# Clustered attention with a fused feed-forward block on one core: first weight sums made ahead of the clips, part of the second ones behind the first products

## The chip, the cores and the metric

The kernel runs on one core of a Trainium2 chip. The metric is the device time of one execution in microseconds (us), lower is better. The core has five engines with queues of their own: TensorE (PE in the profile, its weight loads PEld), VectorE (DVE), ScalarE (ACT), GpSimd (POOL), and SyncE (SP), which issues most transfers. Each takes its instructions in program order; they meet through semaphores.

## The reference

Attention in which a query sees only the keys of its own cluster, followed by a feed-forward block:

```python
q_assign = np.argmax(np.einsum('bhsd,hcd->bhsc', q_n, c_n), axis=-1)   # 16 clusters per head
k_assign = np.argmax(np.einsum('bhsd,hcd->bhsc', k_n, c_n), axis=-1)
mask = q_assign[:, :, :, None] == k_assign[:, :, None, :]
scores = np.where(mask, scale * np.matmul(q, k.transpose(0, 1, 3, 2)), -1e9)
attn = softmax(scores)                       # over the keys, 1e-9 in the denominator
x = np.matmul(attn, v) as (3072, 512)        # 4 batches x 768 tokens, 8 heads x 64
h = x @ w_in                                 # (512, 2048)
g = h * np.clip(h + 3.0, 0.0, 6.0) / 6.0
return g @ w_out                             # (2048, 512)
```

Everything arrives as 64-bit numbers; the kernel rebuilds 32-bit weights from the two halves of each.

## The kernel before

**Stages.** The sixteen pairs of heads are split in two. Pairs 0 to 7 (batches 0 and 1) run as full attention with a cluster mask in steps `n` = 0 to 95, two steps per turn of the loop from line 1284 on. Pairs 8 to 15 run later, with rows sorted by cluster, woven between feed-forward work by a hand-written plan (`late_plan`). The feed-forward block works on 12 blocks of 256 tokens (`B * NHC`); for each there are eight `up` items (first product, item `i` handles the hidden columns `i` and `i + 8` of 128 each) and seven `down` parts (second product, parts 0 to 6).

**Fewer products from sums.** From the second block on, both products use a scheme of seven half-size products in place of eight, which needs sums of weight blocks. The *first weight sums* (`make_first_sums(i)`, one call for each of the eight items) are four VectorE subtractions of 128x256 on `w_in_sb`: three go to a tile `tx` that is stored in DRAM as `td[:, i]` and read again for each later block, the fourth overwrites a block of `w_in_sb`. The first token block still multiplies with the plain `w_in_sb`, so the overwriting subtraction of an item has to come after the first block's use of it. The *second weight sums* (`weight_sums(0..7)`, two halves each of T1, T2, T4 and T3, in this order) are subtractions of 128x1024 on `w_out_sb`; T3 overwrites its source. All 12 blocks' `down` parts use them: part 0 and 1 use T2, part 2 T1, part 3 T3, part 6 T4.

**The first block's items.** Its `up` items run inside the attention loop, the last six of its parts behind it. An item does eight TensorE products into a PSUM tile `ph` (line 597), a lift on ScalarE (line 499), a clip on VectorE (line 502), and with every second item four GpSimd sums of the result (line 635). A counter, `want`, lets them start at n = 60, 64, 70, 74, 80, 84, 90 and 94 (items 0 to 7), and part 0 of `down` at n = 100. Within a turn the item goes ahead of the `prep` steps of the next pair: `turn` (transposes `pqk`, line 320, copied out on ScalarE, line 326) at r = 0 and 2 of the pair's twelve steps, then `cluster_scores`, `route`, and `route_turn` (transposes `po`, line 379). In this stage the tiles `ph`, `pqk`, `pcs`, `pr`, `po` and `pd` share two PSUM slots.

**VectorE in the loop.** Behind the items of a turn come `decode` steps, a list that `share(n, r)` works off: for each of 32 weight chunks `split` (line 232), `join` (238), `power` (248), `rest` (254) and `total` (259), and behind these the eight `weight_sums`. Every sixth step a reciprocal and a multiplication divide one half of a pair's result (lines 473 and 474, `pd` read out of PSUM). GpSimd adds up exponentials (lines 430 and 433, 128x768). Raw weight chunks are loaded by SP with three buffers (line 215).

**The first block's `down` parts.** Each part is eight TensorE products of 128x256 (line 684) into bank `X` or `Y`. `end()` of a part has the eviction: part 1 adds `X` to `y0` (line 691), which frees `X` for part 4; part 3 evicts `Y`, parts 4 and 6 the rest. For the first block the calls of `make_first_sums` stand in front of these evictions: items 7 and 6 at part 0, 5 at part 1, 4 at part 2, 3 and 2 at part 4, 0 at part 5, 1 at part 6.

Of the kernel before, what the change touches and what calls it, by code (L numbers as in the profile page):

```python
# [12 lines left out]
ALU = mybir.AluOpType  # L13
# [15 lines left out]
NFT = DFF // P  # L29
# [90 lines left out]
def fast_path(ctx, tc, ok, q, k, v, centroids, moe_w_in, moe_w_out, out):  # L120
# [3 lines left out]
    nc = tc.nc  # L124
# [53 lines left out]
    st = {}  # L178
# [329 lines left out]
    HF, HC = NFT // 2, DM // 2  # L508
# [30 lines left out]
    def wi(s, t, i):  # L539
        f = t * HF + i  # L540
        return w_in_sb[:, s * HK : (s + 1) * HK, f * P : (f + 1) * P]
# [8 lines left out]
    def make_first_sums(i):  # L550

        tx = txp.tile([P, 3, HK, P], F32, name="tx")
        t1, t2, t4 = (tx[:, k] for k in range(3))
        b11, b12, b21, b22 = wi(0, 0, i), wi(0, 1, i), wi(1, 0, i), wi(1, 1, i)
        for out_, in0, in1 in ((t1, b12, b11), (t2, b22, t1), (t4, b21, t2), (b12, b22, b12)):
            nc.vector.tensor_tensor(out=out_, in0=in0, in1=in1, op=ALU.subtract)  # L556
        nc.sync.dma_start(td[:, i], tx)
        if i < 2:
            st["tx", HF + i] = tx

    def token_sums(b, m):

# [15 lines left out]
    def ffn_items(b):  # L578
        def up(m, i):
            u = (b * NHC + m) * HF + i  # L580
            g = g_sb[:, 0:4, i]
            got = {}

            def begin():
                raise_gates()
                load_block()
                if u >= HF:
                    first_sums(u + 2)
                    halved(b, m, u, i, got)

            def end():
                if u < HF:
                    ph = psum_m.tile([P, 512], F32, name="ph", tag="m")
                    for t in range(2):
                        f = t * HF + i
                        for kt in range(NKT):
                            nc.tensor.matmul(
                                ph[:, t * HC : (t + 1) * HC], lhsT=w_in_sb[:, kt, f * P : (f + 1) * P],
                                rhs=st["xb", b, m][:, kt], start=(kt == 0), stop=(kt == NKT - 1),
                            )  # L600
# [92 lines left out]
        def down(m, part):  # L693
            def keep(chunk, half, y, queue=nc.sync):
                queue.dma_start(out_v[b, 2 * m + chunk][:, half * HC : (half + 1) * HC], y)

            def multiply(second):
                if part < 2:
                    h = range(part * HF // 2, (part + 1) * HF // 2)
                    if second:  # L700
                        product(st["X"], 1, 5, st["T2"], False, True, False, h)
                    else:
                        product(st["X"], 0, 0, wb[0][0], True, False, False, h)
                    return
                kind, bank, half, w = (
                    (4, "Y", 0, st["T1"]), (1, "Y", 1, st["T3"]),
                    (2, "X", 0, wb[1][0]), (6, "Y", 0, wb[1][1]), (3, "Y", 1, st["T4"]),
                )[part - 2]
                h = range(second * HF // 2, (second + 1) * HF // 2)
                product(st[bank], half, kind, w, part == 2, part in (3, 4, 6), part > 3, h)  # L710

            def begin():
                raise_gates()
                if part == 0:
                    st["X"] = psum_m.tile([P, DM], F32, name="X", tag="m")
                    st["y0"] = yp.tile([P, DM], F32, name="y0", tag="y0")
                elif part == 2:
                    st["Y"] = st.get("psum_y", psum_m).tile([P, DM], F32, name="Y", tag="m")
                    st["y1"] = yp.tile([P, DM], F32, name="y1", tag="y1")
                multiply(0)  # L720

            def end():
                multiply(1)
                if part == 0:
                    finish()
                if (b, m, part) == (B - 1, NHC - 1, 6):
                    st["good"] = nc.values_load(ok[0:1, 0:1], min_val=0, max_val=1)
                if part == 4:
                    token_sums(*divmod(b * NHC + m + 1, NHC))
                if (b, m) == (0, 0):  # L730
                    for i in ([HF - 1, HF - 2], [5], [4], [], [3, 2], [0], [1])[part]:
                        make_first_sums(i)
                y0, y1 = st["y0"], st.get("y1")
                if part == 1:
                    nc.scalar.copy(out=y0[:, HC:], in_=st["X"][:, HC:])
                    add(y0[:, HC:], y0[:, HC:], st["X"][:, 0:HC])
                elif part == 3:
                    add(y1[:, 0:HC], y0[:, HC:], st["Y"][:, HC:])
                    add(y1[:, HC:], y1[:, 0:HC], st["Y"][:, 0:HC])
                    keep(1, 1, y1[:, HC:])  # L740
                elif part == 4:
                    nc.scalar.copy(out=y0[:, 0:HC], in_=st["X"][:, 0:HC])
                    keep(0, 0, y0[:, 0:HC])
                elif part == 6:
                    add(y1[:, 0:HC], y0[:, HC:], st["Y"][:, HC:])
                    keep(1, 0, y1[:, 0:HC])
                    add(y0[:, HC:], y0[:, HC:], st["Y"][:, 0:HC])

                    keep(0, 1, y0[:, HC:], nc.scalar if st["last"] else nc.sync)

            return [begin, end]

# [475 lines left out]
    per_batch = NKT * per_pair  # L1228
    total = FIRST * per_pair
    lag_v, lag_d = 2, 4  # L1230
    up_first = NFT // 2

    decode = [step for i in range(NW) for step in decoding_steps(i)]
    decode += [lambda i=i: weight_sums(i) for i in range(8)]
    READY, DECODED = per_batch + 2 * lag_d, 2 * per_batch

    def share(n, r):  # L1240
# [9 lines left out]
    st["early"] = st["free"] = True  # L1250
    st["last"] = st["moving"] = False
    fill, checks = [], []
    st["done"] = 0

    def check_all():
        now, checks[:] = checks[:], []
# [7 lines left out]
    with tc.manual_schedule():  # L1264
# [19 lines left out]
        for n in range(0, total + lag_d + 2, 2):  # L1284
# [10 lines left out]
            m = n - lag_d + 1  # L1295
# [5 lines left out]
            if r == 6:  # L1301
                load(g + 2, "q", "k")
                load(g + 1, "v")
            want = min(max(n + 2 - READY, 0) * up_first // (DECODED - READY) - st["done"], len(fill) // 2)
            st["done"] += want
            for i in range(max(len(prep), want)):
                if i < want:
                    fill.pop(0)()
                    fill.pop(0)()
                if i < len(prep):  # L1310
                    prep[i]()
            if n < total:
                for step in decode[: share(n, r)]:
                    step()
# [388 lines left out]
```

## Time and profile before

| what | value |
|---|---|
| median of 3 runs | 959.21 us (956.59 to 961.89) |
| the profiled execution | 959.56 us, its span 957.8 us |
| TensorE clock granted | 0.998 of full speed |
| PE busy in 0 to 130 us, 130 to 280, 280 to 957.8 | 126.56, 140.31, 662.78 us |
| VectorE busy in the same stretches | 108.50, 131.89, 353.97 us |
| first block's items on PE | 136.4 to 238.8 us |
| first block's `down` parts on PE | 242.7 to 270.3 us |

The program's span is 1.8 us shorter than the time measured for the same execution. The first row of the table is what later runs are compared with. A row of the views that follow has a start in us, a duration in us, the engine, the line, the operation, and output<-input; in square brackets stands how long the engine sat idle before it and what released it.

### The profile page before, as it was taken

The page shows a single profiled execution, that of the slowest core. Times are in us where ns is not written, and L with a number is a line of the kernel's source. Part 1 is how long each engine was busy: PE and PEld are TensorE (multiplying, and loading weights), DVE is VectorE, ACT ScalarE, POOL GpSimd, SP SyncE. Part 2 cuts the span into 40 slices and gives each one's busy share as a digit, 9 for nine tenths or more (in the row PEclk, how much of TensorE's full clock was granted, in tenths as well). Part 3 has the DMA queues.
Part 4 walks back from the last instruction along what each step waited for, and adds up shares of the span by engine and source line. Part 5 has one row for each costly group of instructions (what it writes and reads, how often), then busy time and mean ns, then how long its engine had stood idle before and what let it go on. Part 6 is the DMA issues. An engine that isn't in the chain of part 4 may idle for free.

```text
span 957.8 us, 17621 instructions
## 1 busy us (share of the span) xinstructions
PE 929.6 (97%) x6358; PEld 725.5 (76%) x6358; DVE 594.4 (62%) x1306; ACT 349.8 (37%) x731; POOL 576.3 (60%) x1302
## 2 busy tenths in 40 slices
PE   8999999999899999999999999999999999999997
PEld 5444445555698798787897988888888799999996
DVE  6789888989977276274483474374471564636261
ACT  6888877765112232222232231241331311202020
POOL 3877767657367577776777878767777160303030
PEclk9999999999999999999999999999999999999999
DMA  7255464350474557456584484654744333323210
GB/s 206 90 133 155 132 176 124 106 145 10 145 223 137 151 159 164 129 130 153 153 198 119 120 204 118 160 155 114 198 142 95 102 96 116 102 72 105 66 57 26
DMA packets 174351, 124.23 MB, mean 130 GB/s; under 512 B 134064, under 2 KB 152496, under 8 KB 174256
## 3 DMA queue, kind: packets, MB, share of 16 engines
q1 hardware_dynamic: 164320, 109.86, 42.7%
q0 software_dynamic: 9216, 12.60, 4.4%
q8 instruction: 52, 0.85, 0.4%
q10 hardware_dynamic: 720, 0.56, 0.2%
q14 instruction: 43, 0.35, 0.1%
HBM read 94.67 MB, written 28.31 MB: 128 GB/s over the span
## 4 chain that ended last, share of the span: by engine, by line
PE 67%; DVE 3%; DMA 2%; issue 1%; ACT 0%; SPq 0%; another core or an unknown queue 0%; ACTq 0%; DVEq 0%
PE Y L684 17%; PE uY L645 15%; PE X L684 12%; PE uX L645 11%; PE pv L1096 3%; PE ps L899 3%; PE ps L1057 3%; DMA piece<-qd 2%; PE pv L1057 1%; PE pd L1120 1%; PE pcs L337 1%; PE rk L981 1%; PE ps L1137 1%; DVE tx L556 0%; DVE w_out_sb L523 0%
## 5 line engine op out<-in xcount | busy, mean ns | idle before, releaser
L433 POOL TENSOR_TENSOR acc<-acc,ex 128x768 f32<-128x768 f32 x64 | 123.3, 1927 | 37.4 <-ACT ex L423 33.9
L1014 POOL DMA_INDIRECT qd<-qn,pos x96 | 96.2, 1002 | 54.8 <-issue 17.5
L1030 POOL DMA_INDIRECT xn<-xsd,pos x96 | 94.3, 982 | 46.0 <-ACT sx L499 24.3
L499 ACT ACTIVATE sx<-g_sb,half_c 128x512 f32<-128x512 f32 x88 | 63.8, 725 | 146.5 <-DVE g_sb L656 126.3
L635 POOL TENSOR_TENSOR g_sb<-g_sb 128x256 f32<-128x256 f32 x52 | 41.8, 825 | 122.1 <-DVE g_sb L502 121.1
L1014 POOL DMA_INDIRECT kvd<-kvn,pos x96 | 96.1, 1001 | 27.3 <-issue 25.4
L1006 POOL MEMSET w_low<- 128x1 f32 x864 | 91.3, 106 | 33.3
L691 DVE TENSOR_TENSOR y<-y,Y 128x256 f32<-128x256 f32 x48 | 20.2, 421 | 132.7 <-PE Y L684 131.9
L684 PE MATMUL X<-w_out_sb,g_sb 128*128 128x256 f32 x384 | 90.4, 382 | 4.0 <-DVE y L691 2.2
L645 PE MATMUL uX<-xb,w_in_sb 128*128 128x128 f32 x704 | 93.0, 275 | 0.0
L684 PE MATMUL Y<-T,g_sb 128*128 128x256 f32 x384 | 88.0, 381 | 0.0
L684 PE MATMUL Y<-w_out_sb,g_sb 128*128 128x256 f32 x384 | 87.7, 380 | 0.0
L645 PEld LDWEIGHTS uX<-xb,w_in_sb 128*128 128x128 f32 x704 | 85.7, 192 | 0.0
L684 PEld LDWEIGHTS X<-w_out_sb,g_sb 128*128 128x128 f32 x384 | 70.9, 190 | 18.5 <-issue 4.0
L684 PEld LDWEIGHTS Y<-T,g_sb 128*128 128x128 f32 x384 | 72.1, 190 | 13.2 <-issue 3.9
L684 PEld LDWEIGHTS Y<-w_out_sb,g_sb 128*128 128x128 f32 x384 | 71.9, 190 | 10.6 <-issue 1.3
L656 DVE TENSOR_TENSOR sx<-uX,sx 128x128 f32<-128x128 f32 x176 | 51.1, 290 | 45.9 <-ACT sx L663 30.8
L400 PE MATMUL ps<-xf 64*128 64x384 f32 x384 | 78.5, 487 | 0.6 <-ACT ex L423 0.6
L423 ACT ACTIVATE ex<-ps 128x768 f32<-128x768 f32 x96 | 72.6, 802 | 4.5 <-PE ps L400 4.5
L443 PE MATMUL pv<-ex,vt 128*64 128x384 f32 x384 | 72.5, 499 | 0.0
L502 DVE SCALAR_TENSOR_TENSOR g_sb<-sx,g_sb 128x512 f32<-128x512 f32 x88 | 63.9, 728 | 3.3 <-ACT sx L499 2.3
L656 DVE TENSOR_TENSOR g_sb<-uY,sx 128x128 f32<-128x128 f32 (+1 forms) x176 | 65.6, 414 | 0.0
(194 smaller groups left out, 1796.7 us busy)
## 6 DMA issues: line engine op xcount, KB each, us to landing
tx<-td SPq DMA_DIRECT2D x86, 384.0 KB
raw<-in_moe_w_in_dram SPq DMA_DIRECT2D x16, 512.0 KB
raw<-in_moe_w_out_dram SPq DMA_DIRECT2D x16, 512.0 KB
xb<-xd SPq DMA_DIRECT2D x12, 512.0 KB
out_dram<-y SPq DMA_DIRECT2D x44, 128.0 KB
qk<-in_q_dram SPq DMA_DIRECT2D x18, 192.0 KB
qk<-in_k_dram SPq DMA_DIRECT2D x18, 192.0 KB
vt<-in_v_dram SPq DMA_DIRECT2D x16, 192.0 KB
```

Of the source, the lines that this page charges most:

```text
L400: nc.tensor.matmul(st["ps", n][:, t, 0:HALF], lhsT=x[r, NCH + j], rhs=x[r, hf * NHC : (hf + 1) * NHC], start=first, stop=last, skip_group_ ...
L423: nc.scalar.activation(out=ex, in_=sc, func=ACT.Exp, scale=SM_SCALE)
L433: nc.gpsimd.tensor_tensor(out=acc, in0=acc, in1=ex, op=ALU.add)
L443: nc.tensor.matmul(pv[t * D : (t + 1) * D], lhsT=vt[:, t, j], rhs=ex[:, t], start=(j == 0), stop=(j == NCH - 1),)
L499: nc.scalar.activation(out=r, in_=h, func=ACT.Relu, bias=half_c, scale=1.0 / 6.0)
L502: nc.vector.scalar_tensor_tensor(out=g, in0=r, scalar=1.0, in1=h, op0=ALU.min, op1=ALU.mult)
L645: nc.tensor.matmul(dst, lhsT=w[:, kt], rhs=x(kt), start=(kt == 0), stop=(kt == HK - 1))
L656: nc.vector.tensor_tensor(out=out_, in0=in0, in1=in1, op=ALU.add)
L684: nc.tensor.matmul(bank[:, half * HC : (half + 1) * HC], lhsT=g_sb[:, kind, i], rhs=w[:, i], start=(first and i == 0), stop=(last and i == ...
L1006: nc.gpsimd.memset(w_low, W_LOW)
L1014: i = nc.gpsimd.indirect_dma_start(out=rows[name, g, t], in_=src, in_offset=None, out_offset=bass.IndirectOffsetOnAxis(ap=pos[:, a, j, t : ...
L1030: nc.gpsimd.indirect_dma_start(out=xn[:, j, t], out_offset=None, in_=rows["xsd", g, t], in_offset=bass.IndirectOffsetOnAxis(ap=pos[:, 0, j ...
```

## The change

1. `make_first_sums(i)` is split: `kept_sums(i)` does the three subtractions into `tx` and stores it, the fourth stays in `make_first_sums`, which calls `kept_sums` only for an item that hasn't had it. `kept_sums` of items 7, 6, 5 and of 4 and 3 is issued in `end()` of the first block's `up` items 0, 1, 2 and 5 (`sooner`), ahead of the item's products and so of its clip in VectorE's queue.
2. The last four `weight_sums` (both halves of T4 and of T3) leave the decode list. T3's halves are made at the end of parts 0 and 1 of the first block's `down`, T4's at the end of parts 2 and 3.
3. In `end()` of the first block's parts, the sums now follow the evictions.
4. The counter `want` gives way to a list of steps, `up_at`. Item 3 goes from n = 74 to n = 72. Where a turn of the loop has two `turn` steps (r = 0: n = 60, 72, 84), the first of them is issued ahead of the item, the second behind it; before, the item was ahead of both.

```diff
+    def subtract(out_, in0, in1):
+        nc.vector.tensor_tensor(out=out_, in0=in0, in1=in1, op=ALU.subtract)
+    def kept_sums(i):
         tx = txp.tile([P, 3, HK, P], F32, name="tx")
         t1, t2, t4 = (tx[:, k] for k in range(3))
-        b11, b12, b21, b22 = wi(0, 0, i), wi(0, 1, i), wi(1, 0, i), wi(1, 1, i)
-        for out_, in0, in1 in ((t1, b12, b11), (t2, b22, t1), (t4, b21, t2), (b12, b22, b12)):
-            nc.vector.tensor_tensor(out=out_, in0=in0, in1=in1, op=ALU.subtract)
+        for sums in ((t1, wi(0, 1, i), wi(0, 0, i)), (t2, wi(1, 1, i), t1), (t4, wi(1, 0, i), t2)):
+            subtract(*sums)
         nc.sync.dma_start(td[:, i], tx)
         if i < 2:
             st["tx", HF + i] = tx
+        st["kept"].add(i)
+    def make_first_sums(i):
+        if i not in st["kept"]:
+            kept_sums(i)
+        subtract(wi(0, 1, i), wi(1, 1, i), wi(0, 1, i))
...
             def end():
                 if u < HF:
+                    for other in sooner.get(u, ()):
+                        kept_sums(other)
                     ph = psum_m.tile([P, 512], F32, name="ph", tag="m")
...
-                if (b, m) == (0, 0):
-                    for i in ([HF - 1, HF - 2], [5], [4], [], [3, 2], [0], [1])[part]:
-                        make_first_sums(i)
                 y0, y1 = st["y0"], st.get("y1")
...
+                if (b, m) == (0, 0):
+                    for i in ([HF - 1, HF - 2], [5], [4], [], [3, 2], [0], [1])[part]:
+                        make_first_sums(i)
+                    if part in (0, 1):
+                        weight_sums(6 + part)
+                    elif part in (2, 3):
+                        weight_sums(2 + part)
...
-    decode += [lambda i=i: weight_sums(i) for i in range(8)]
+    decode += [lambda i=i: weight_sums(i) for i in range(4)]
+    st["kept"] = set()
+    sooner = {0: (7,), 1: (6,), 2: (5,), 5: (4, 3)}
+    up_at = (60, 64, 70, 72, 80, 84, 90, 94, 100)
...
-            want = min(max(n + 2 - READY, 0) * up_first // (DECODED - READY) - st["done"], len(fill) // 2)
-            st["done"] += want
-            for i in range(max(len(prep), want)):
-                if i < want:
-                    fill.pop(0)()
-                    fill.pop(0)()
-                if i < len(prep):
-                    prep[i]()
+            if len(prep) > 1:
+                prep.pop(0)()
+            if n in up_at:
+                fill.pop(0)()
+                fill.pop(0)()
+            for step in prep:
+                step()
```

More of the change, by code (lines that the diff above doesn't have):

```diff
@@ L548, in first_sums @@
             nc.sync.dma_start(tx, td[:, i])
-    def make_first_sums(i):
+    def subtract(out_, in0, in1):
+        nc.vector.tensor_tensor(out=out_, in0=in0, in1=in1, op=ALU.subtract)
+    def kept_sums(i):
         tx = txp.tile([P, 3, HK, P], F32, name="tx")
         t1, t2, t4 = (tx[:, k] for k in range(3))
-        b11, b12, b21, b22 = wi(0, 0, i), wi(0, 1, i), wi(1, 0, i), wi(1, 1, i)
-        for out_, in0, in1 in ((t1, b12, b11), (t2, b22, t1), (t4, b21, t2), (b12, b22, b12)):
-            nc.vector.tensor_tensor(out=out_, in0=in0, in1=in1, op=ALU.subtract)
+        for sums in ((t1, wi(0, 1, i), wi(0, 0, i)), (t2, wi(1, 1, i), t1), (t4, wi(1, 0, i), t2)):
+            subtract(*sums)
         nc.sync.dma_start(td[:, i], tx)
@@ L1230, in fast_path @@
     lag_v, lag_d = 2, 4
-    up_first = NFT // 2
     decode = [step for i in range(NW) for step in decoding_steps(i)]
-    decode += [lambda i=i: weight_sums(i) for i in range(8)]
+    decode += [lambda i=i: weight_sums(i) for i in range(4)]
+    st["kept"] = set()
+    sooner = {0: (7,), 1: (6,), 2: (5,), 5: (4, 3)}
+    up_at = (60, 64, 70, 72, 80, 84, 90, 94, 100)
     READY, DECODED = per_batch + 2 * lag_d, 2 * per_batch
@@ L1252, in fast_path @@
     fill, checks = [], []
-    st["done"] = 0
     def check_all():
```

## The prediction

> **What bounds the kernel now.** I read the page's head first, then TensorE's waits, then its order of time around the change, then VectorE's.
>
> ```profile
> span 957.8 us, 17621 instructions
> ...
> PE 929.6 (97%) x6358; PEld 725.5 (76%) x6358; DVE 594.4 (62%) x1306; ACT 349.8 (37%) x731; POOL 576.3 (60%) x1302
> ```
>
> TensorE is busy for 97% of the span, and no edit removes a product. So the change can win only TensorE's idle time, and only where it touches it, between 130 and 280 us. The list of TensorE's waits (total, times, longest, in us) names what is there to win:
>
> ```profile
> PE X L684 <- DVE y L691: 2.2, 1, 2.2
> PE X L684 <- DVE g_sb L502: 1.8, 1, 1.8
> ...
> PE pqk L320 <- ACT xf L326: 1.6, 2, 0.8
> ...
> PE pqk L320 <- DVE rcp L473: 0.7, 1, 0.7
> ...
> PE uX L645 <- DVE sx L656: 0.4, 1, 0.4
> PE po L379 <- DVE rcp L473: 0.4, 1, 0.4
> ```
>
> In TensorE's order of time these are the places:
>
> ```profile
> 141.39 0.66 PE L320 MATMUL pqk<-ident,qk 128*128 128x128 f32 x4 [0.82 <-ACT xf L326]
> ...
> 173.39 1.09 PE L320 MATMUL pqk<-ident,qk 128*128 128x128 f32 x8
> ...
> 178.22 3.72 PE L597 MATMUL ph<-xb,w_in_sb 128*128 128x256 f32 x16
> 182.69 0.66 PE L320 MATMUL pqk<-ident,qk 128*128 128x128 f32 x4 [0.75 <-DVE rcp L473]
> ...
> 198.76 0.49 PE L379 MATMUL po<-ident_q,one_hot 128*128 128x128 bf16 x6 [0.38 <-DVE rcp L473]
> ...
> 242.73 1.99 PE L684 MATMUL X<-w_out_sb,g_sb 128*128 128x256 f32 x8 [1.82 <-DVE g_sb L502]
> ...
> 253.19 3.62 PE L684 MATMUL Y<-w_out_sb,g_sb 128*128 128x256 f32 x16
> 259.02 1.99 PE L684 MATMUL X<-w_out_sb,g_sb 128*128 128x256 f32 x8 [2.21 <-DVE y L691]
> ```
>
> Together 2.21 + 1.82 + 1.64 + 0.75 + 0.41 + 0.38 = 7.2 us: the most this change can take off TensorE's path. Four of these six waits end on VectorE. Its order of time shows why, and where it has room:
>
> ```profile
> 140.90 0.69 DVE L502 SCALAR_TENSOR_TENSOR g_sb<-g_sb,ph 128x512 f32<-128x512 f32 x1 [2.30 <-ACT g_sb L499]
> ...
> 154.80 0.69 DVE L502 SCALAR_TENSOR_TENSOR g_sb<-g_sb,ph 128x512 f32<-128x512 f32 x1 [2.15 <-ACT g_sb L499]
> ...
> 170.15 0.69 DVE L502 SCALAR_TENSOR_TENSOR g_sb<-g_sb,ph 128x512 f32<-128x512 f32 x1 [1.18 <-ACT g_sb L499]
> ...
> 173.65 0.69 DVE L238 SCALAR_TENSOR_TENSOR wtop<-raw,wtop 128x512 uint32<-128x512 uint32 x1
> ...
> 175.11 2.15 DVE L254 SCALAR_TENSOR_TENSOR wunit<-raw,wunit 128x512 f32<-128x512 uint32 x1
> ...
> 180.08 2.55 DVE L473 RECIPROCAL rcp<-pd 128x384 f32<-128x384 f32 x1
> ...
> 196.16 2.55 DVE L473 RECIPROCAL rcp<-pd 128x384 f32<-128x384 f32 x1
> ...
> 207.57 0.69 DVE L259 TENSOR_TENSOR w_out_sb<-wtop,wunit 128x512 f32<-128x512 f32 x1
> 211.57 0.69 DVE L502 SCALAR_TENSOR_TENSOR g_sb<-g_sb,ph 128x512 f32<-128x512 f32 x1 [3.31 <-ACT g_sb L499]
> ...
> 228.63 0.69 DVE L502 SCALAR_TENSOR_TENSOR g_sb<-g_sb,ph 128x512 f32<-128x512 f32 x1 [0.51 <-ACT g_sb L499]
> ...
> 230.29 2.78 DVE L523 TENSOR_TENSOR T<-w_out_sb 128x1024 f32<-128x1024 f32 x1
> ...
> 239.72 2.35 DVE L523 TENSOR_TENSOR T<-w_out_sb,T 128x1024 f32<-128x1024 f32 x2
> 241.99 0.68 DVE L502 SCALAR_TENSOR_TENSOR g_sb<-g_sb,ph 128x512 f32<-128x512 f32 x1
> 242.59 2.88 DVE L523 TENSOR_TENSOR T<-w_out_sb,T 128x1024 f32<-128x1024 f32 x2
> 245.39 3.41 DVE L523 TENSOR_TENSOR w_out_sb<-w_out_sb 128x1024 f32<-128x1024 f32 x2
> 248.72 2.54 DVE L473 RECIPROCAL rcp<-pd 128x384 f32<-128x384 f32 x1
> ...
> 258.55 0.41 DVE L691 TENSOR_TENSOR y<-y,X 128x256 f32<-128x256 f32 x1
> ```
>
> The reader is to see two things. The clips wait for their lifts, and leave VectorE gaps of 2.30, 2.15, 1.18 and 3.31 us, exactly at the items that get early sums. And between the gaps it has none: from 170.15 to 208 us no row has a bracket, and from 211.57 to 242.67 only 0.51 us is free. Where the first product starts is VectorE's end of that chain (241.99 + 0.68), not TensorE's.
>
> A third fact lies in durations. T1's halves take 2.78 us and T2's 2.35 / 2 = 1.2, for the same shape:
>
> ```profile
> 166.46 3.89 POOL L433 TENSOR_TENSOR acc<-acc,ex 128x768 f32<-128x768 f32 x2 [1.86 <-ACT ex L423]
> 174.89 1.81 POOL L430 TENSOR_TENSOR acc<-ex 128x768 f32<-128x768 f32 x1 [4.53 <-ACT ex L423]
> ...
> 230.18 8.54 POOL L433 TENSOR_TENSOR acc<-acc,ex 128x768 f32<-128x768 f32 x4 [3.33 <-ACT ex L423]
> ```
>
> T1's first half began 0.1 us after a GpSimd add and lasted about such an add (1.81) longer than T2's. The 2.15 us row of line 254 ends 0.56 us after the GpSimd add that had begun just ahead of it at 174.89; its neighbours of the same size take 0.69. So a VectorE operation with both inputs in SBUF, which meets a running GpSimd add, waits for that add to end: 0 to 1.8 us each. All moved sums are of this kind.
>
> **Part by part.**
>
> *Order of `turn` and item (n = 60, 72, 84).* The second `turn` waited for the first one's copy, queued behind the lift: 0.82 us, twice. Now the item's 3.7 us lie between the two, and the copy needs 0.6: minus 0.82 at 60 and at 84. At n = 74 the third `turn` waited 0.75 for the reciprocal; with item 3 gone from there it waits for item 3's clip, long done: minus 0.75.
>
> *Fifteen early subtractions* of 128x256:
>
> ```profile
> L556 DVE TENSOR_TENSOR tx<-w_in_sb,tx x16: 424/425/490, 252.3 to 270.7; 128x256 f32<-128x256 f32 x16
> L556 DVE TENSOR_TENSOR tx<-w_in_sb x8: 413/419/420, 251.8 to 269.8; 128x256 f32<-128x256 f32 x8
> ```
>
> 0.42 + 2 x 0.425 = 1.27 us for one item, 6.3 for five. Alone they fit the gaps (1.27 in 2.30 and 2.15, 1.27 in 1.18, 2.55 in 3.31), so nothing to 0.1 us is the lower end. With a GpSimd add in the way each gap costs up to 1.8 more: 4 x 1.8 = 7.2 less the spare 1.03 + 0.88 + 0.76 = 4.5 us, the upper end. At item 2 I take the waiting case, since the row at 166.46 covers that gap until 170.35: clip at about 170.75 (0.6 later than before, though its lift comes 0.8 earlier). At item 0 and 1 the add ends early enough. The five stores of `tx` join SP's queue ahead of raw weight loads, which wait for VectorE's line 254 anyway and run two chunks (7 us of decoding) ahead; I cost them at nothing, and with the cover gone at one subtraction's delay each, 1.3 us.
>
> *Item 3 at n = 72.* VectorE reaches this clip behind the row at 173.65, so at 174.4 + 0.6 = 175.0. TensorE issues the item at 173.39 - 0.82 + 0.55 = 173.1, ends at 176.8; the lift takes 0.7 more: 177.6. VectorE stands for 2.6 us where it had no gap, and behind it wait six decode steps and the reciprocal: 177.6 + 0.6 + 6 x 0.72 + 0.4 of GpSimd's delay = 182.9 instead of 180.08. The clip no longer comes after it (0.6), so the chain is 2.3 us late from here; its ends are 0 (if line 254's 1.5 us of waiting at 175.11 is saved on top of the other gains) and 3.5.
>
> *Reciprocal at 196.16.* It ends 2.3 later, at 201.0. TensorE is there 0.82 + 0.75 = 1.57 us earlier than its 198.38, so its 0.38 grows to 4.2: the gains so far go into this wait, and TensorE is 2.3 late.
>
> *Item 5 (n = 84).* The lift ended where the clip began, at 211.5, and ends at 211.5 + 2.3 + 0.6 (the `turn` ahead of the item) = 214.4; VectorE is free at 208.3 + 2.3 = 210.6 and needs 2.55, with a GpSimd add 4.4: clip between 214.4 and 215.0, 3.0 late. The 0.51 gap takes its share: 2.5 late. T1's two waits (2.78 - 1.21 = 1.57 each) were almost the longest possible; shifted against GpSimd by 1 us I take the mean, half of 1.8, which gives back 1.4. The first product starts 1.1 us late; its ends are minus 4.6 (VectorE in time: 2 x 0.82, 0.75, 0.38 and 1.82 all won) and plus 6.6 (rival C).
>
> *T3 and T4 behind the first products, evictions first.* 2.88 + 3.41 us leave the queue ahead of the reciprocal at 248.72 and of the add at 258.55, and so do sums of items 7, 6 and 5. New queue from the first product's start: reciprocal and multiplication 3.1, two overwriting sums 0.85, T3's first half 1.7, the small set-up operations 1.9, then the add, ending at 8.0 us. Part 4 needs it at 253.19 + 3.45 - 242.73 = 13.9: the 2.21 us vanish. T3's second half is done by 10.2 and needed at 12.2, T4's by about 17, needed at 20.9; these covers are thin for T3 only.
>
> *Part 6.* Item 1's sums (1.7 us) now stand behind the last eviction and ahead of the next block's additions, where they were ahead of both: these start about 2.5 us after the block's first product instead of 2.0, and item 2's reload stands behind item 1's store in SP's queue. The 0.41 us wait stays and grows: I take plus 0.3, ends minus 0.4 and plus 1.
>
> Sum: 1.1 - 2.2 + 0.3 = -0.8 us against 959.56. That execution lies 0.35 above the median, so I name 958.4 for a median. Behind 280 us TensorE hardly waits for this stage, and I carry the shift to the end.
>
> **The rivals.**
>
> *B, all waits go.* VectorE's lateness stays under 1 us because the moved operations meet no adds: minus 5 to 7.2, 952 to 954.2. For it: the sums' length fits the gaps. Against: the gap that item 3 opens, which no earlier work fills.
>
> *C, VectorE becomes the bound of the attention stage.* The early sums lose a whole add at each of four gaps (4.5 us), item 3's gap adds 2.6, and the first product starts 7.1 - 0.5 = 6.6 us late; with 2.2 given back and 0 to 1 for part 6, plus 4.4 to 5.4: 963.6 to 964.6. It decides from 7 us of lateness on. For it: the row at 166.46; against: one add per gap, often over early. The Trainium skill ("SBUF — State Buffer", Who interferes with whom) has the rule behind it: a VectorE instruction with two SBUF inputs and a GpSimd one reading SBUF exclude each other for the whole instruction. The T1 rows agree (2.78 against 1.2).
>
> *D, the wait moves only.* T3's second half misses its 2.0 us of cover, and part 3 waits instead of part 4: plus 1.4, 960.6. GpSimd's sums of item 7 run in that stretch and could hold T3 up.
>
> **How the numbers follow.** Forecast 0.59, B 0.18, C 0.12, D 0.11. I call 0.5% (4.8 us) the least that can be told from no change: under 954.4 faster, over 964.0 slower. B gives 0.17 faster, C 0.09 slower, the rest lies within: 0.74. The range goes from B's middle, 953.8, to short of C, 962.6.
>
> **What would show it.** Right: `pqk` without waits at n = 60, 74 and 84; a gap of 2 to 3 us before item 3's clip; `po` waiting about 4 us for a reciprocal; no wait of `X` for line 691's add. Wrong: the `po` wait under 1 us (B's sign), clips 3 us or more behind their lifts (C), a wait of `Y` for T3 (D), or a moved time in stretches behind 300 us, which nothing here explains.

## The result, and the profile after

| us | kernel before | kernel after |
|---|---|---|
| median (lowest to highest), 7 executions each | 959.23 (956.59 to 961.89) | 954.56 (953.32 to 956.97) |
| the profiled execution | 959.56 | 955.15 |
| its span | 957.8 | 953.4 |

The ratio of after to before is 0.995, with a 95% interval of 0.9933 to 0.9966: 4.7 us less, where 0.8 were forecast. The interval leaves out 1; by the bound that the prediction set for telling a change (0.5%, 4.8 us) it lies just within, and near the lower end of the range.

The list of TensorE's waits in the profile after (total, times, longest, in us) answers to the one shown of before:

```profile
PE ph L607 <- DVE one_hot L357: 2.3, 1, 2.3
...
PE X L694 <- DVE g_sb L502: 1.8, 1, 1.8
...
PE uX L655 <- DVE sx L666: 0.6, 1, 0.6
```

The waits of `pqk` and that of `X` for the late add (line 701 now) are gone, the 1.8 us ahead of the first product are untouched, and 2.3 us are new. In TensorE's order of time (start, duration, waits in brackets):

```profile
140.29 0.60 PE L320 MATMUL pqk<-ident,qk 128*128 128x128 f32 x4
144.62 0.66 PE L320 MATMUL pqk<-ident,qk 128*128 128x128 f32 x4
...
173.17 3.62 PE L607 MATMUL ph<-xb,w_in_sb 128*128 128x256 f32 x16
...
180.97 0.66 PE L320 MATMUL pqk<-ident,qk 128*128 128x128 f32 x4
...
195.35 5.38 PE L607 MATMUL ph<-xb,w_in_sb 128*128 128x256 f32 x16 [2.33 <-DVE one_hot L357]
...
243.69 1.99 PE L694 MATMUL X<-w_out_sb,g_sb 128*128 128x256 f32 x8 [1.82 <-DVE g_sb L502]
...
257.61 1.89 PE L694 MATMUL X<-w_out_sb,g_sb 128*128 128x256 f32 x8
...
275.67 0.68 PE L655 MATMUL uX<-xs,tx 128*128 128x128 f32 x4 [0.65 <-DVE sx L666]
```

The sixteen products at 195.35 took 5.38 us, not 3.72. Windows of 2 us show why: the granted clock (third number from the end) was halved from 196 us to a little over 199.

```profile
194.00:196.00 2.00, 0.65 (x3) 0.63 (x4) 1.93 (x6) 0.00 (x0) 1.47 (x1) 1.00 0.99 320
196.00:198.00 2.00, 2.00 (x7) 1.56 (x6) 1.97 (x3) 0.00 (x0) 0.00 (x0) 0.50 1.34 258
198.00:200.00 2.00, 2.00 (x8) 1.64 (x7) 1.91 (x2) 0.00 (x0) 0.00 (x0) 0.64 1.15 271
```

VectorE's order of time after, at the clips that got early sums, at item 3's clip, and at the one-hots behind it:

```profile
138.44 2.04 DVE L551 TENSOR_TENSOR tx<-w_in_sb 128x256 f32<-128x256 f32 x1
...
141.31 0.68 DVE L502 SCALAR_TENSOR_TENSOR g_sb<-g_sb,ph 128x512 f32<-128x512 f32 x1
...
171.46 0.68 DVE L502 SCALAR_TENSOR_TENSOR g_sb<-g_sb,ph 128x512 f32<-128x512 f32 x1
...
177.55 0.69 DVE L502 SCALAR_TENSOR_TENSOR g_sb<-g_sb,ph 128x512 f32<-128x512 f32 x1 [1.90 <-ACT g_sb L499]
...
182.42 2.55 DVE L473 RECIPROCAL rcp<-pd 128x384 f32<-128x384 f32 x1
...
194.58 0.62 DVE L357 TENSOR_TENSOR one_hot<-pr,mx 128x192 bf16<-128x192 f32 x2
...
197.17 2.55 DVE L473 RECIPROCAL rcp<-pd 128x384 f32<-128x384 f32 x1
...
210.68 2.38 DVE L551 TENSOR_TENSOR tx<-w_in_sb,tx 128x256 f32<-128x256 f32 x2
...
214.23 0.68 DVE L502 SCALAR_TENSOR_TENSOR g_sb<-g_sb,ph 128x512 f32<-128x512 f32 x1
```

The one-hots that in after start at 194.58 stood in before at

```profile
192.31 0.62 DVE L357 TENSOR_TENSOR one_hot<-pr,mx 128x192 bf16<-128x192 f32 x2
```

Where did 4.4 us of span come from? Two steps that both kernels issue in the same order, the turn of `dn` and the first product of the second block's T2, stood in the first profile of before at

```profile
407.05 0.49 PE L1133 MATMUL pdt<-ident,dn 128*128 128x128 f32 x3
...
418.47 0.87 PE L899 MATMUL ps<-ident,piece 128*128 128x128 f32 x6 [1.26 <-ACT xnat L900]
421.73 0.85 PE L337 MATMUL pcs<-xnat,cnT 128*32 128x384 f32 x8 [0.60 <-ACT xnat L900]
434.77 0.84 PE L899 MATMUL ps<-ident,piece 128*128 128x128 f32 x6 [0.56 <-issue]
436.08 1.91 PE L684 MATMUL X<-T,g_sb 128*128 128x256 f32 x8
```

and in that of after at

```profile
405.20 0.49 PE L1147 MATMUL pdt<-ident,dn 128*128 128x128 f32 x3
...
429.60 0.85 PE L913 MATMUL ps<-ident,piece 128*128 128x128 f32 x6 [0.15 <-issue]
430.91 1.91 PE L694 MATMUL X<-T,g_sb 128*128 128x256 f32 x8
```

So after is 407.05 - 405.20 = 1.85 us ahead at the first and 5.17 at the second. Up to 405 us after has gained 1.85, but only 1.3 of it by 296 us; the other 0.6 arose near 300 us, where this profile of before is that much slower than the second one shown below. Another 3.3 came in 30 us of work that no edit touches. At the end the lead is 4.4: in after a second stretch at half clock follows on the wait of 2.09 us at 611 us (a wait, and the windows behind it), which before had too, without such a stretch.

```profile
611.41 0.84 PE L913 MATMUL ps<-ident,piece 128*128 128x128 f32 x6 [2.09 <-DMA piece<-qd]
```

```profile
612.00:614.00 2.00, 2.00 (x18) 1.97 (x17) 0.62 (x2) 0.80 (x1) 1.71 (x5) 0.61 1.09 280
614.00:616.00 2.00, 2.00 (x12) 2.00 (x11) 0.00 (x0) 0.00 (x0) 1.74 (x5) 0.54 1.04 261
```

### The profile page after: what moved, and what is told of

Same layout as the page of the kernel before. It is cut to its first block, busy times and chain, and to the rows that moved or that the text cites. A ratio compares the mean times of both kernels' runs of the same rounds, so it can differ in the third digit from the quotient of the medians.

```text
span 953.4 us, 17615 instructions
## 1 busy us (share of the span) xinstructions
PE 930.6 (98%) x6358; PEld 728.2 (76%) x6358; DVE 595.6 (62%) x1306; ACT 349.7 (37%) x731; POOL 574.6 (60%) x1302
## 4 chain that ended last, share of the span: by engine, by line
PE 69%; DMA 2%; issue 1%; DVE 1%; SPq 0%; POOL 0%; ACT 0%
PE Y L694 17%; PE uY L655 15%; PE X L694 13%; PE uX L655 11%; PE pv L1110 3%; PE ps L913 3%; PE ps L1071 3%; DMA piece<-qd 2%; PE pv L1071 1%; PE pd L1134 1%; PE pcs L337 1%; PE ps L1151 1%; PE rk L995 0%; PE pdt L1147 0%; DVE y L701 0%
## 5 line engine op out<-in xcount | busy, mean ns | idle before, releaser
L645 POOL TENSOR_TENSOR g_sb<-g_sb 128x256 f32<-128x256 f32 x52 | 38.0, 754 | 125.5 <-DVE g_sb L502 124.5
L1028 POOL DMA_INDIRECT kvd<-kvn,pos x96 | 95.6, 996 | 25.7 <-issue 24.7
```

What stands on the lines that cost most here:

```text
L1028: i = nc.gpsimd.indirect_dma_start(out=rows[name, g, t], in_=src, in_offset=None, out_offset=bass.IndirectOffsetOnAxis(ap=pos[:, a, j, t : ...
```

## The experiments

Theory W: the gain is what the removed waits between 130 and 280 us bring, less VectorE's lateness. For the 3.3 us behind 405 us there are two: theory S, that the passage is slow in before whenever it runs and any shift of the stage ahead shortens it, and theory O, that it is a thing of single executions. Each set ran on one chip, with the kernel before beside it; the three sets ran on three chips. All differences are of medians within a set.

| kernel | median, us | before beside it, us | ratio (95%) |
|---|---|---|---|
| order alone | 958.46 | 957.03 | 1.0017 (1.0007 to 1.0028) |
| early sums alone | 952.17 | 957.03 | 0.9959 (0.9945 to 0.9974) |
| T3, T4 and evictions alone | 954.92 | 957.03 | 0.9986 (0.9976 to 0.9996) |
| after, second time | 954.70 | 956.48 | 0.9981 (0.997 to 0.9992) |
| after, item 3 at n = 74 | 953.04 | 956.48 | 0.997 (0.9959 to 0.9982) |
| the same, half of T2 behind the clip | 951.84 | 956.48 | 0.9954 (0.9941 to 0.9967) |
| after without T3, T4, evictions | 953.85 | 956.48 | 0.9979 (0.9969 to 0.9988) |
| after, third time | 954.90 | 960.40 | 0.9957 (0.9937 to 0.9977) |
| order, sums, n = 74, half of T2 | 955.77 | 960.40 | 0.9951 (0.993 to 0.9973) |
| the same with T3, T4 moved | 955.40 | 960.40 | 0.9954 (0.9937 to 0.9972) |
| early sums and half of T2 | 956.62 | 960.40 | 0.9964 (0.9947 to 0.998) |

### Before once more

No edit.

> The kernel before, profiled once more. Two theories of where 4.4 us came from: the profile of before and after differ by 1.9 us up to 400 us (waits removed between 130 and 280 us, less VectorE's lateness), and by 3.6 us more in a passage from 406 to 438 us, which no edit touches. Theory S (the passage is systematic): in before, the passage's waits come back in this profile (xnat 1.26, pcs 0.60, ps 0.56 us, and PE's products there 3 us longer than in after), span near 957.8. Theory O (one-off): the passage of 406 to 438 us is about 3 us shorter here than in the first profile of before, and the span is near 954.5 to 955, or the 3 us turn up somewhere else.

955.83 us, span 954.0. TensorE's order of time in this second profile of before:

```profile
406.40 0.49 PE L1133 MATMUL pdt<-ident,dn 128*128 128x128 f32 x3
...
415.63 0.82 PE L899 MATMUL ps<-ident,piece 128*128 128x128 f32 x6
418.16 0.85 PE L337 MATMUL pcs<-xnat,cnT 128*32 128x384 f32 x8
430.99 0.85 PE L899 MATMUL ps<-ident,piece 128*128 128x128 f32 x6 [0.34 <-DMA piece<-qd]
432.30 1.91 PE L684 MATMUL X<-T,g_sb 128*128 128x256 f32 x8
```

From one landmark to the other 25.90 us, against 29.03 in the first profile and 25.71 in after: the waits for `xnat` are not there, and with them go 3.1 us. Theory O holds for the profile. Against this profile, after is ahead by 406.40 - 405.20 = 1.2 us at the first landmark and 1.39 at the second, and by 0.6 in the span, for its second stretch at half clock, behind 611 us, takes some back.

### Parts of the change alone

The order alone, against before (the loop over `prep` as in after):

```diff
-    up_first = NFT // 2
+    up_at = (60, 64, 70, 72, 80, 84, 90, 94, 100)
...
-            want = min(max(n + 2 - READY, 0) * up_first // (DECODED - READY) - st["done"], len(fill) // 2)
...
+            if len(prep) > 1:
+                prep.pop(0)()
+            if n in up_at:
+                fill.pop(0)()
+                fill.pop(0)()
+            for step in prep:
+                step()
```

> Before with one part of the change alone: the order of turn and item at n = 60, 72 and 84, with item 3 at n = 72. Not in it: early sums, T3 and T4 behind the first products, evictions first. Theory W (waits): the pqk waits of 0.82, 0.82 and 0.75 us go, item 3's clip makes VectorE 2 us late, the first product starts 0.5 to 1.3 us later than in before, and the wait of 2.21 us for the add of the second half stays: offset at 290 us +0.5 to +1.3, time 959.5 to 960.5 us. Theory S adds: the passage from 406 to 438 us gets 3 us shorter by any shift of the stage ahead of it, so 956.5 to 957.5. Theory O: the passage comes or goes whatever the shift.

1.4 us slower than before. TensorE's order of time:

```profile
195.41 5.38 PE L597 MATMUL ph<-xb,w_in_sb 128*128 128x256 f32 x16 [2.33 <-DVE one_hot L357]
...
243.75 1.99 PE L684 MATMUL X<-w_out_sb,g_sb 128*128 128x256 f32 x8 [1.82 <-DVE g_sb L502]
...
260.04 3.50 PE L684 MATMUL X<-w_out_sb,g_sb 128*128 128x256 f32 x8 [2.21 <-DVE y L691]
```

The three `pqk` waits are gone, and all of it is paid back at n = 80, by the wait and the half clock behind it; the late add's wait of 2.21 us stays, and here it too is followed by half clock (3.50 us for 1.99). The first product starts 1.0 us late, as theory W had it; at 290 us the kernel is 2.0 us behind before, where W had 0.5 to 1.3, since W had no second stretch at half clock. Theory S's gain did not come.

The early sums alone, against before (`kept_sums` and the two-step `make_first_sums` as in after):

```diff
+    st["kept"] = set()
+    sooner = {0: (7,), 1: (6,), 2: (5,), 5: (4, 3)}
...
+                    for other in sooner.get(u, ()):
+                        kept_sums(other)
                     ph = psum_m.tile([P, 512], F32, name="ph", tag="m")
```

> Before with one part of the change alone: the kept first sums of items 7, 6, 5, 4 and 3 made ahead of the clips of items 0, 1, 2 and 5. Theory W: the three pqk waits stay (0.82, 0.82, 0.75 us), item 3's clip brings no gap, the first product starts 0 to 1 us later, and behind it 3.8 us of subtractions are gone from VectorE's queue ahead of the late add: its wait of 2.21 us goes. Offset at 290 us -1.2 to -2.2, 957 to 958 us. Theory S adds another -3: 954 to 955 us.

4.9 us faster than before, more than theory W had. In its order of time the `pqk` waits are there, the first product starts 0.3 us later than in the second profile of before, and the products from there on run without a wait:

```profile
141.61 0.66 PE L320 MATMUL pqk<-ident,qk 128*128 128x128 f32 x4 [0.82 <-ACT xf L326]
...
243.08 1.99 PE L694 MATMUL X<-w_out_sb,g_sb 128*128 128x256 f32 x8 [1.82 <-DVE g_sb L502]
...
253.54 3.62 PE L694 MATMUL Y<-w_out_sb,g_sb 128*128 128x256 f32 x16
256.99 1.89 PE L694 MATMUL X<-w_out_sb,g_sb 128*128 128x256 f32 x8
```

The spans differ by 954.0 - 950.2 = 3.8 us, and the stretch between the landmarks is the same in both (25.80 and 25.90), so theory S is not needed. At 290 us the lead is 2.7 us, in the main the 2.21 us ahead of the second half of `X` and the 0.41 us of the second block's first `uX`; the last 1.1 us come behind 430 us, in work that no edit touches.

That the medians differ by more than the spans is in part half clock. The span times one minus the granted clock says, roughly, what an execution lost to it, since the clock is on record to 0.001, which is 1 us; in the fourteen profiles 1.0 to 2.1 us of that lie behind the last product. Averaged over the executions of this set, before lost 3.0 us (clock 0.9968) and the early sums 1.6 (0.9983): of the 4.9 us some 1.4, by this estimate, is fewer stretches at half clock.

T3, T4 and the evictions alone, against before:

```diff
-    decode += [lambda i=i: weight_sums(i) for i in range(8)]
+    decode += [lambda i=i: weight_sums(i) for i in range(4)]
...
-                if (b, m) == (0, 0):
-                    for i in ([HF - 1, HF - 2], [5], [4], [], [3, 2], [0], [1])[part]:
-                        make_first_sums(i)
                 y0, y1 = st["y0"], st.get("y1")
...
+                if (b, m) == (0, 0):
+                    for i in ([HF - 1, HF - 2], [5], [4], [], [3, 2], [0], [1])[part]:
+                        make_first_sums(i)
+                    if part in (0, 1):
+                        weight_sums(6 + part)
+                    elif part in (2, 3):
+                        weight_sums(2 + part)
```

> Before with one part of the change alone: the four half sums of T3 and T4 behind the first products, and the evictions ahead of the first block's sums. Theory W: nothing changes up to the first product (same offset to 0.1 us at 242 us); behind it 6.3 us of sums leave VectorE's queue ahead of the late add, whose wait of 2.21 us goes; the sums of items 2 to 7 still stand there. Offset at 290 us -1.7 to -2.2, 957 to 957.5 us. Theory S adds another -3: 954 to 954.5 us.

2.1 us faster. The wait for the late add is gone, and two others have come:

```profile
256.07 1.99 PE L684 MATMUL Y<-w_out_sb,g_sb 128*128 128x256 f32 x8 [0.70 <-DVE w_out_sb L523]
...
276.78 0.68 PE L645 MATMUL uX<-xs,tx 128*128 128x128 f32 x4 [1.48 <-DMA tx<-td]
```

The first is the wait of the prediction's rival D, `Y` for T3's second half: without the early sums, those of items 7, 6 and 5 stand whole ahead of it. The second is for the reload of an item's sums, which by the code stands in SP's queue behind the stores of `tx`. In the trace the kernel is level with the second profile of before again behind 277 us, and its span is 1.0 us shorter; the 2.1 of the medians is more. That a wait of 2.21 us can bring half clock in some executions of before (last section) would fit, and so does the granted clock, 0.9977 on average against before's 0.9968 (2.2 and 3.0 us lost); where in them the half clock lies isn't known, since one execution in each run was profiled.

So the parts sum to 1.4 - 4.9 - 2.1 = -5.6 us, and the whole was worth 1.8 on the next chip. One reason is that the early sums and the moved T3 and T4 win the same 2.21 us; without the second of them the sum is still -3.5, and the rest is of the size by which sets differ.

### After, and one edit in it

No edit.

> The changed kernel once more, beside the kernel before on one chip. The second profile of before has no slow passage at 406 to 438 us, and its span is 954.0 us, 0.6 above the 953.4 of after, whose profile holds two stretches of half TensorE clock of 3.41 us each (behind the waits of 2.33 us at 195 us and of 2.09 us at 611 us; 1.66 us lost in each). Theory O (the first 3.6 us of the difference belong to that one profile, and the rest of the 4.7 us between the medians to how often executions hold such stretches): the median is 0.5 to 2.5 us under that of before, ratio 0.9975 to 0.9995, and executions without a half-clock stretch (mean clock 0.999) are 1.2 to 1.9 us under those of before. Theory S (the gain is 4.7 us everywhere): ratio 0.994 to 0.996 again.

1.8 us faster than before: theory O's range. The profile repeats both half-clock stretches, behind the products at 195.43 and 612.63 us. The expectation's other number missed: the one execution at a granted clock of 0.999 took 952.35 us, and before's at that clock 955.5 in the median, 3.2 more where 1.2 to 1.9 were named. Averaged over the set, after lost 3.5 us to half clock (0.9964) and before 2.3 (0.9976), so on this chip the change pays back some 1.2 us that way.

Item 3 back at n = 74, against after:

```diff
-    up_at = (60, 64, 70, 72, 80, 84, 90, 94, 100)
+    up_at = (60, 64, 70, 74, 80, 84, 90, 94, 100)
```

> After with item 3 back at n = 74, the rest as in after. Theory W (item 3 ahead of its turn opens a gap on VectorE, which makes the reciprocal of n = 80 late and TensorE wait 2.33 us, long enough for a half-clock stretch): the wait of 2.33 us at 195 us is gone or under 0.5 us, no half-clock stretch near 196 us, mean clock 0.998 to 0.999 in most executions; the pqk wait of 0.75 us comes back or is covered by the turn order; first product within 0.4 us of before; time 4 to 6 us under before, like the kernel with the early sums alone (4.9). Rival (item 3's place is worth the 0.75 us it saves): 0.3 to 0.8 us slower than after.

3.4 us faster than before, less than the 4 to 6 named, and 1.7 faster than after beside it. VectorE has no gap ahead of this clip, and its reciprocal is on time; TensorE now waits for that reciprocal at `pqk`:

```profile
179.98 2.55 DVE L473 RECIPROCAL rcp<-pd 128x384 f32<-128x384 f32 x1
...
183.11 0.68 DVE L502 SCALAR_TENSOR_TENSOR g_sb<-g_sb,ph 128x512 f32<-128x512 f32 x1
```

```profile
182.59 0.66 PE L320 MATMUL pqk<-ident,qk 128*128 128x128 f32 x4 [1.30 <-DVE rcp L473]
...
194.57 3.72 PE L607 MATMUL ph<-xb,w_in_sb 128*128 128x256 f32 x16
...
241.56 1.99 PE L694 MATMUL X<-w_out_sb,g_sb 128*128 128x256 f32 x8 [1.82 <-DVE g_sb L502]
```

The wait at 195 us is gone, with its half clock. The first product starts 1.2 us ahead of before (242.79 in the second profile), where I had expected it level: so the order of `turn` and item is worth something at n = 60 and 84, and item 3's place was what spent it.

The second half of T2 behind the clip of the first block's last item, on top:

```diff
+                    if u == HF - 1:
+                        weight_sums(3)
...
-    decode += [lambda i=i: weight_sums(i) for i in range(4)]
+    decode += [lambda i=i: weight_sums(i) for i in range(3)]
```

> After with item 3 at n = 74 and the second half of T2 behind the clip of the first block's last item. The wait of 1.82 us ahead of the first product ends on that clip, which stands in VectorE's queue behind T2's two halves of 1.2 us each. Theory V (VectorE's queue sets the first product): the wait falls to 0.6 us, and time to 1.2 us under the kernel without this edit, 5.5 to 7 under before. Rival (T2's half is then late for its own product, 6 us on): a wait of X for T of about 1 us takes its place, and the time stays.

```profile
240.42 1.99 PE L696 MATMUL X<-w_out_sb,g_sb 128*128 128x256 f32 x8 [0.68 <-DVE g_sb L502]
```

The wait fell from 1.82 to 0.68 us, nothing took its place, and the time fell by 1.2 us: theory V, though the intervals of the two kernels overlap. At 951.84 us this is the fastest of that set, 4.6 us under before (5.5 to 7 were named) and 2.9 under after.

After without T3, T4 and the evictions' place (the third diff above, undone):

> After without one part: T3 and T4 are made among the decoding steps and the first block's sums ahead of the evictions, as in before; the order of turn and item and the early sums stay. Theory R (the early sums alone take 3.8 us from VectorE's queue ahead of the late add, so T3 and T4 need not move): the wait of 2.21 us stays away, offset at 270 us within 0.4 of after's, time within 0.5 us of after. Theory W (both are needed): a wait of 0.5 us or more for the late add, and 0.5 to 2 us slower than after.

0.85 us faster than after (953.85 against 954.70), and in TensorE's order of time the first `X` of part 4 has no wait:

```profile
254.21 3.62 PE L694 MATMUL Y<-w_out_sb,g_sb 128*128 128x256 f32 x16
257.66 1.89 PE L694 MATMUL X<-w_out_sb,g_sb 128*128 128x256 f32 x8
```

The intervals overlap, and the difference is above the 0.5 us that theory R allowed, but it is not slower. Theory R: beside the early sums the moved T3 and T4 win nothing.

### The last set

After, unchanged, a third time:

> The changed kernel a third time beside the kernel before, for the size of the effect: the first set gave a ratio of 0.995, the second 0.9981 [0.997, 0.9992]. Theory O (the true gain is 1 to 2.5 us, and the first set's before was slow for another reason): ratio 0.9973 to 0.999 again, before's median 955.5 to 958. Theory S (the effect is nearer 4.7 us, and the second set was odd): ratio under 0.9965. Clock: behind each wait of TensorE over 2.04 us which lies whole in one of the 3.41 us stretches in which the clock record is divided, a stretch at half clock; behind none of 1.88 us or less.

The ratio, 0.9957, is that of theory S, while its reason is not: after took what it took before (954.56, 954.70, 954.90 in three sets), and before differs, 959.23, 956.48 and 960.40. The expectation had named 955.5 to 958 for before; that missed. Half clock explains little of that: before's granted clock averages 0.9976 where it took 956.48 us and 0.9970 here, which is 0.6 us, and after's in this set is 0.9970 too. In this profile of after no stretch is at half clock, though TensorE waits as long as in the others:

```profile
196.28 3.69 PE L607 MATMUL ph<-xb,w_in_sb 128*128 128x256 f32 x16 [2.36 <-DVE one_hot L357]
```

The kernel with the order at n = 60 and 84, the early sums, item 3 at n = 74 and half of T2 behind the clip, but T3, T4 and evictions as in before; against the kernel of 951.84 us:

```diff
-    decode += [lambda i=i: weight_sums(i) for i in range(3)]
+    decode += [lambda i=i: i == 3 or weight_sums(i) for i in range(8)]
...
+                if (b, m) == (0, 0):
+                    for i in ([HF - 1, HF - 2], [5], [4], [], [3, 2], [0], [1])[part]:
+                        make_first_sums(i)
                 y0, y1 = st["y0"], st.get("y1")
...
-                if (b, m) == (0, 0):
-                    for i in ([HF - 1, HF - 2], [5], [4], [], [3, 2], [0], [1])[part]:
-                        make_first_sums(i)
-                    if part in (0, 1):
-                        weight_sums(6 + part)
-                    elif part in (2, 3):
-                        weight_sums(2 + part)
```

> Order of turn and item at n = 60 and 84, the early sums, item 3 at n = 74, the second half of T2 behind the last item's clip; T3 and T4 and the sums ahead of the evictions as in before. Theory R (T3 and T4 need no move, and the evictions' place costs 0.3 to 0.6 us in part 6): 0.4 to 1 us under the kernel with T3 and T4 moved (which was 4.6 under before), so 5 to 6 under before. Rival (T4 and T3 in VectorE's queue ahead of the late add, now 1.1 us earlier, bring a wait back): 3 to 4.5 under before.

4.6 us under before, between the ranges of theory R and its rival; it cannot be told from after beside it.

The same with T3 and T4 behind the first products again, so that against the kernel of 951.84 us only the first block's sums have moved ahead of the evictions:

```diff
+                if (b, m) == (0, 0):
+                    for i in ([HF - 1, HF - 2], [5], [4], [], [3, 2], [0], [1])[part]:
+                        make_first_sums(i)
                 y0, y1 = st["y0"], st.get("y1")
```

> As the last kernel, but T3 and T4 behind the first products, as in after. Only the first block's sums stand ahead of the evictions, as in before. Theory E (the evictions' place alone makes the second block's first uX wait): that wait falls from 0.65 to 0.41 us or less, and the time is 0.2 to 0.6 us under the kernel with evictions first (4.6 under before). Rival (the order of sums and evictions is worth nothing): 4.3 to 4.8 under before.

5.0 us under before, theory E's range. The second block's first `uX` has no wait at all in its trace; it was 0.38 us in the kernel of 951.84 us and 0.65 in after, so the evictions' place did make it. The time cannot tell it.

The early sums alone with half of T2 behind the clip, against the kernel with the early sums alone:

```diff
+                    if u == HF - 1:
+                        weight_sums(3)
...
-    decode += [lambda i=i: weight_sums(i) for i in range(8)]
+    decode += [lambda i=i: i == 3 or weight_sums(i) for i in range(8)]
```

> Before with the early sums and the second half of T2 behind the last item's clip, and nothing else: no other order of turn and item, T3 and T4 in place. Theory V (VectorE's queue sets the first product, so the three pqk waits that the order saves are worth nothing here): as fast as the kernel with that order to 0.5 us, 5.5 to 6.5 under before. Rival (the order's 1.6 us count in full): 3.5 to 4.5 under before.

3.8 us under before, in the range of the rival. Up to 246 us its trace lies 1.3 us behind that of the kernel with the order (first product at 241.78 and 240.50 us): the order counts, and theory V fell here by the trace. In time it is 0.85 us slower than that kernel, within the noise.

What blurred this set is the passage behind 405 us. Between the two landmarks the fourteen profiles of the study took 25.7 to 26.3 us, but for four: 29.03 (before, the first), 27.43, 28.94 and 28.92 (these last three kernels). TensorE's order in the last of them shows the same first wait as the first profile of before:

```profile
403.41 0.49 PE L1145 MATMUL pdt<-ident,dn 128*128 128x128 f32 x3
...
414.87 0.87 PE L911 MATMUL ps<-ident,piece 128*128 128x128 f32 x6 [1.38 <-ACT xnat L912]
```

## Why the prediction was right and where it was not

- **Two slips of reading.** Five of the six rows of TensorE's waits end on VectorE, not four; the lower end of the range, 953.8, is not the middle of rival B, which is 953.1. The median of 954.56 us lies in the range with either.
- **The `pqk` waits** went, all three, as worked out.
- **Early sums.** At items 0 and 5 they fit. A GpSimd add held a sum up at both (2.04 us at 138.44, where I had taken the add to end early enough, and 2.38 for two at 210.68), and the clips still stood within 0.25 us of their lifts' ends. At items 1 and 2 VectorE came late to the sums, and the clips stood 1.1 and 2.05 us behind their lifts; at item 2 the sums met no add, but line 254's operation ahead of them did, and the clip came at 171.46, 0.7 later than named. TensorE waited for none of these clips. Those at 177.55 (item 3) and 214.23 (item 5) came where 177.6 and 214.4 to 215.0 were named.
- **Item 3.** The gap of 1.90 us (2.6 named) and the reciprocal at 182.42 (182.9) were right. The lateness reached TensorE as forecast, but one step sooner: not `po`, which did not wait at all (by the prediction's list, rival B's sign), but `ph`, which takes the PSUM buffer that the one-hots read. They came 194.58 - 192.31 = 2.27 us later, and the wait was 2.33, not 4.2; half clock behind it then cost 1.7 more, for which the prediction had no term. The reciprocal behind it was only 1.0 late, because line 254's operation ahead of it met no GpSimd add this time (0.69 us, 1.96 in before).
- **The first product** came 243.69 - 242.73 = 0.96 us late where I named 1.1, for another reason, so the match is luck. T1's halves still met their adds (2.78 and 2.83 us), so the 1.4 us that I gave back were not there. Nor was VectorE's lateness: from 2.7 us at the clip of 214.23 it had worked itself down to TensorE's own 1 us at the next clip, which waits for its lift. That 1 us is the half clock's: in the third profile of after, without it, the products at n = 80 start 0.93 us later than in the first (the whole execution lay 0.9 later from its first 30 us on) and the first product 0.10 earlier (243.59 us). Half clock apart, the first product is level with before.
- **T3, T4 and part 6.** The 2.21 us vanished and part 6's wait grew by 0.24 (0.3 named). That T3 and T4 were needed for it was wrong: the early sums do it alone.
- **The size.** The sum of -0.8 us against the 1.2 ahead of the second profile of before, at 405 us, is a fair fit, but with the luck of the first product in it: in the third profile of after, with no stretch at half clock, the lead over that profile grows by 2.0 us between 29 and 290 us. Of the 4.7 us measured, the sum gives a sixth. The step that failed is "Behind 280 us TensorE hardly waits for this stage, and I carry the shift to the end". It took the passage from 405 to 436 us as a fixed length, and in the very execution from which I worked it is 3.1 us longer than in the next; in after's three profiles it is not. The text had named "a moved time in stretches behind 300 us" as what would show it wrong, and that is what came.

How much of the 4.7 us is the change's own stays open in part. On the chip where before took 956.48 it is 1.8 us, and about 3 without the difference in half clock, an estimate from the clocks given above; no profile of before was taken there, and the waits that make the gain are read against a profile of before from another chip. Where before took 959.23 and 960.40, the difference is 4.7 and 5.5, and the one profile of before from those executions (of the first) has the slow passage. That the passage makes the rest is argued from that one profile and from the three late ones, of other kernels; why it comes and goes is not settled, and that after is spared it always is not either (three of its twelve executions in the last set took 959.1 to 961.6 us). In the slow profiles ScalarE's copies of `uX` start later behind their products than in the others, and the copy to `xnat` is late by that; what delays them was not found.

## What to carry to other kernels

Before an offset is carried to the end, see whether the work behind it takes the same time in a second profile of the same kernel: 3 us of passage can hide a change of 1 to 2. A step is best moved into a gap that its engine already has (the early sums: 4.9 us alone, in the one set where they ran so); moved to where the engine must wait for a younger result, it opens a gap and makes all behind it late (item 3: 1.7 us lost). When two edits aim at one wait, try each alone, since the second may only cost.

## What the runs showed of the hardware

The half clock has a sharp rule. All changes of the clock in one execution's record lie on a grid of 3.413 us that starts anew in each execution. In the fourteen profiles TensorE had nine waits of 1.92 to 2.34 us that lay whole between two lines of this grid; each was followed by exactly one stretch at half clock, from the next line on. Twelve waits of 1.96 to 2.36 us had such a line within them, and none was; nor were seven whole ones of 1.81 to 1.88 us. With all idle time of TensorE in each such window added up, from the first line to the last product, the profiles divide in the same way: 1.92 us and more in nine windows, each followed by half clock, and 1.88 or less in all others, none followed by it. So the same wait costs its length in one execution and 1.7 us more in another (195.35 and 196.28 above), and shortening a wait to under 1.9 us can be worth more than its length. The Trainium skill ("TensorE: Matmul & The Clock Gate", Part 1 on the clock gate, and "HAM oscillation — how this bites in real kernels") has the free-running window of 3413 ns, with which the trace agrees. Its rule that idle gaps over about 3.4 us throttle differs: here 1.92 us inside one window were enough.

The kernel before took 957.03, 956.48 and 960.40 us in the median of 23 and 24 executions on three chips, and after 954.56 to 954.90 in its three sets: the measured gain changed threefold from set to set.
